# Attention in quarter-array matmuls: scores as 64 x 32, the product with v as 64 x 64, without zero padding

## The chip, the cores and the metric

The kernel runs on one core of a Trainium2 chip. A core has TensorE for matrix multiplication (its matmul side is called PE in the rows, its weight loads PEld), VectorE (DVE), ScalarE (ACT), GpSimd (POOL) and SyncE (SP), which issues the DMAs. TensorE writes to PSUM, which has eight banks of 512 fp32 columns on 128 partitions; the other engines read the results from there. The metric is the time of one execution in microseconds (us), and lower is better. Three executions of the kernel before took 828.35, 829.13 and 830.47 us; the median is 829.13.

## The reference

Attention over 4 batches, 8 heads, 576 positions and 64 dimensions a head, then two dense layer pairs on 2304 tokens of 512:

```python
scores = scale * np.matmul(q, k.transpose(0, 1, 3, 2))
rel = pos[:, None] - pos[None, :]
mask_plain = (rel >= 0) & (rel < 32)
mask_dil = (rel >= 0) & (rel < 128) & (rel % 4 == 0)
# heads 0 to 3 use mask_plain, heads 4 to 7 use mask_dil
scores = np.where(masks, scores, -1e9)
attn = np.exp(scores - max); attn = attn / (sum + 1e-09)
x = np.matmul(attn, v)                    # then (2304, 512)
x = elu(x @ w_in) @ w_out                 # 512 -> 2048 -> 512
x = h * clip(h + 3, 0, 6) / 6 @ w2_out    # h = x @ w2_in
```

A query sees only 32 keys, either the last 32 or every fourth of the last 128. All is fp32.

## The kernel before

**Units.** Attention is cut into 18 units of 128 tokens with all eight heads. The host lays the queries out in blocks of 32 rows, each with a window of 64 keys: four blocks of consecutive positions for the plain heads and four blocks of every fourth position for the dilated ones, eight blocks (`NB`) for each of four heads of a kind. A block of one head is thus 32 queries by 64 keys by 64 dimensions. The kernel packs them into larger matmuls with zeros: the 128 rows of `q` hold two heads' dimensions, with the two heads' queries in different columns and zeros in between, so that one matmul of 128 rows gives two heads' scores (64 columns of queries, 64 of keys). `scores` (L571) makes 16 such matmuls into one bank `ps`. `low` (L583) scales and masks them on VectorE, `top` (L591) takes the row minimum, `expos` (L611) the exponentials on ScalarE, `norm` and `scale` (L619, L623) divide by the sum. `turn` (L626) transposes the result in four TensorE transpositions into a bank `pp`. `turned` (L633) copies it to `pt` in two halves of 64 partitions, each into other columns; the rest of `pt` was set to zero once (L1499) and stays zero. `pv` (L642) multiplies with `v`, again 16 matmuls on 128 rows, into a bank `po`, which `x_hi` and `x_lo` (L655, L658) read out as a high and a low part, or `whole` (L719) for the last six units.

**The first four units** take another way through the same steps (`full`, `pe_masks`): the mask is added in the bank by bf16 matmuls with `minus`, a scaled identity (`masked`, L564), and the maximum and the difference are taken from PSUM (`less`, L597).

**The two layer pairs.** `tile1` (L764) runs the first pair on 512 tokens at a time: a block of 12 matmuls of 128 x 512 into a bank h0 or h1 (`gemm1`, L752), the ELU on ScalarE and VectorE, and 12 matmuls into the four banks y0 to y3 (`g2`, L806). They need three passes each, since every number is split into two fp32r parts. The last 768 tokens of the first pair and all of the second run later (L1109, L1163, L1353) and read nothing of attention's banks or buffers. The weights are loaded as raw 64-bit numbers and converted on ScalarE and VectorE (L335 to L377), and weight sums of the second pair are formed beside the first one's matmuls.

**The order** is made by a planner (L108 to L196). Each piece of work is a job with a key, a table of costs by engine and what it needs; the planner keeps a clock for each engine, picks for each the ready job with the lowest key unless a later one starts earlier by its cost, and emits it. Rings of slots stand for buffers: a job that takes a slot waits for the planned end of the slot's last users. Scores, transposition and product of a unit each take one bank in turn, by `bank_tags` (L513): in the first four units from a0, a1 and y0 to y3, later from the ring "a" (a0 and a1) alone. The first four units stand at the start, the next four among the first 512 tokens' matmuls, the other ten behind. What an engine does is in this fixed order; at run time it waits on semaphores. Until 46 us of its clock the planner fills TensorE's idle time with matmuls of the identity (`fill`, L1484).

Of the kernel before, what the change touches and what calls it, by code (L numbers as in the profile page):

```python
# [42 lines left out]
    LEAD=10.0,  # L43
# [6 lines left out]
    BUFS=dict(y=4, ghl=3, q=1, k=1, v=1, pt=1, g=8, w=6, o=9),  # L50
# [16 lines left out]
class Slot:  # L67

    def __init__(self, tag=None):
        self.tag, self.users = tag, ()  # L70

# [127 lines left out]
def tile_window_attention_two_mlps(  # L199
# [45 lines left out]
    mask = at.tile([P, 5, KW], BF16, name="mask")  # L245
# [17 lines left out]
    RINGS = {n: Ring(SIZES.get(n, 1)) for n in (*SIZES, "p0", "p1")}  # L263
# [4 lines left out]
    RINGS["all"] = Ring(list(BANKS.values()))  # L268
    RINGS["ghl"] = Ring([Slot(f"ghl{n}") for n in range(SIZES["ghl"])])
# [242 lines left out]
    pts = [at.tile([P, NB // 2, HH, 2 * QB], F32, name=f"pt{z}") for z in range(SIZES["pt"])]  # L512
    bank_tags = deque(["a", "y0", "a", "y1", "y2", "y3"])  # L513
# [6 lines left out]
    def unit(u, key, step):  # L520
# [3 lines left out]
        for n, src, shape, us, dk in (  # L524
            ("q", q_in, [P, 2, NB, KW], 1.3, 0), ("k", k_in, [P, k_in.shape[2]], 1.1, 0),
# [13 lines left out]
        masks = [first_seen(u * QB, S // DIL)] * DIL + [first_seen(u * UN + n * QB, S) for n in range(UN // QB)]  # L539
        tags = []  # L540
        for _ in range(3):
            tags.append(bank_tags[0] if u < U1 else "a")
            bank_tags.rotate(-1)
        r = {}

        def bank(k, shape, nm):
            r[nm] = ps.tile(shape, F32, tag=bu[k].tag, name=f"{nm}{u}")
            return r[nm]

        def window(n):  # L550
            if n < DIL:
                return t["k"][:, 2 * (UN + WIN):].rearrange("p (c r z) -> p c r z", c=2, r=DIL)[:, :, n]
            n -= DIL
            return t["k"][:, 0:2 * (UN + WIN)].rearrange("p (c z) -> p c z", c=2)[:, :, n * QB:n * QB + KW]

        runs = []
        while sum(w for _, w, _ in runs) < NB:
            n = sum(w for _, w, _ in runs)
            runs.append((n, next(w for w in range(NB - n, 0, -1) if len(set(masks[n:n + w])) == 1), masks[n]))

        full = u < CFG["FULL"]
        pe_masks = u < CFG["MPE"]

        def masked(e):  # L564
            pe = bank(0, [P, NB, KW], "ps")
            for n, w, z in runs:
                nc.tensor.matmul(
                    pe[:, n:n + w, :], minus, mask[:, z:z + 1, :].to_broadcast([P, w, KW]), start=(n == 0), stop=False
                )

        def scores(e):  # L571
            pe = r["ps"] if pe_masks else bank(0, [P, NB, KW], "ps")
# [3 lines left out]
            for n in range(NB):  # L576
                kk = window(n)
                for c in range(2):
                    nc.tensor.matmul(
                        pe[c * KW:(c + 1) * KW, n, :], t["q"][:, c, n, :], kk[:, c], start=not pe_masks, stop=not pe_masks or n == NB - 1  # L580
                    )

        def low(e):  # L583

            for n, w, z in runs:
                nc.vector.scalar_tensor_tensor(
                    out=r["s"][:, n:n + w, :], in0=r["ps"][:, n:n + w, :], scalar=-SCALE,
                    in1=mask[:, z:z + 1, :].to_broadcast([P, w, KW]), op0=ALU.mult, op1=ALU.add,
                )

        def top(e):  # L591
            if pe_masks:
                nc.vector.tensor_reduce(out=r["mx"], in_=r["ps"], axis=AX.X, op=ALU.max)
# [3 lines left out]
        def less(e):  # L597
            nc.vector.tensor_tensor(
                out=r["s"], in0=r["ps"], in1=r["mx"].to_broadcast([P, NB, KW]), op=ALU.subtract
            )  # L600
# [10 lines left out]
        def expos(e):  # L611
            x, z = (r["ps"], SCALE) if pe_masks else (r["s"], -1.0)
            for n in range(NB):
                nc.scalar.activation(  # L614
                    out=r["s"][:, n, :], in_=x[:, n, :], func=AF.Exp, scale=z, bias=r["mx"][:, n],
                    accum_out=r["sm"][:, n],
# [9 lines left out]
        def turn(e):  # L626
            pp = bank(1, [P, NB // 2, P], "pp")
            for m in range(0, NB, 2):
                nc.tensor.transpose(pp[:, m // 2, :], r["s"][:, m:m + 2, :].rearrange("p n k -> p (n k)"), ident)

        pt = pts[u % len(pts)]

        def turned(par):  # L633
            def fn(e):
                rows = slice(par * KW, (par + 1) * KW)
                copy(
                    e, pt[rows, :, :, par * QB:(par + 1) * QB],
                    r["pp"][rows].rearrange("p m (h i) -> p m h i", i=QB),
                )
            return fn  # L640

        def pv(e):  # L642

            po = bank(2, [P, KD, UN], "po")
            for m in range(NB // 2):
                for h in range(HH):
                    o = po[h % 2 * D:(h % 2 + 1) * D]
                    if m < DIL // 2:
                        o = o[:, 2 + h // 2].rearrange("p (i r) -> p r i", r=DIL)[:, 2 * m:2 * m + 2]
                    else:  # L650
                        n = 2 * m - DIL
                        o = o[:, h // 2, n * QB:(n + 2) * QB]
                    nc.tensor.matmul(o, t["v"][:, m, h, :], pt[:, m, h, :], start=True, stop=True)  # L653
# [978 lines left out]
```

## Time and profile before

| | |
|---|---|
| median of three runs | 829.13 us |
| the profiled execution | 829.3 us, span 827.6 us |
| PE busy | 811.6 us (98%) |
| DVE, ACT busy | 636.3 us (77%), 505.5 us (61%) |
| DMA | 230.49 MB, mean 279 GB/s |
| first matmul of the first layer | 29.47 us |
| last product with v | begins at 278.49 us |

The busy time of PE counts each matmul to its modelled end, and neighbours overlap, so that gaps shorter than a matmul's drain don't show in it. The chain of waits shows from start to start instead. Names are those of the program: `ps` scores, `pp` transposed exponentials, `pt` their copy, `po` product with v, `h` and `yp` the banks of the first layer pair. A line can be that of a helper: L276 is every copy, L279 every difference, L335 to L346 the conversion of raw weights. The granted clock was 1.00 in all stretches.

### The profile page before, as it was taken

The numbers are of one execution on the slowest core, as the hardware profiler recorded it, in microseconds if no ns is written. First come the engines' busy times: TensorE is split into PE (matmuls) and PEld (weight loads), VectorE is DVE, ScalarE is ACT, GpSimd is POOL, SyncE is SP. The second block draws the span as 40 slices with busy tenths as digits, with TensorE's granted clock in tenths as the row PEclk, the third lists the DMA queues.
The fourth block names the chain that finished last, engine by engine and source line by source line (L and its number), as shares of the span: only waits on it lengthen the run. The fifth ranks groups of instructions, "written<-read, shape, count | busy, mean of one in ns | idle before, by whom it ended". The sixth has DMA issues, their size and how long they took to land.

```text
span 827.6 us, 15806 instructions
## 1 busy us (share of the span) xinstructions
PE 811.6 (98%) x5691; PEld 750.5 (91%) x5691; DVE 636.3 (77%) x1310; ACT 505.5 (61%) x1179; POOL 47.6 (6%) x71
## 2 busy tenths in 40 slices
PE   8899999999999999999999999999999999999998
PEld 7788888888877887999999999999999999999998
DVE  5999898877778787677998675797677896555985
ACT  2999975766676655677786554444555445444452
POOL 2000010001001000100000000100001100002001
PEclk9999999999999999999999999999999999999999
DMA  9999557866888736999779998986999915778323
GB/s 355 408 408 367 195 180 246 271 213 228 261 287 294 243 125 216 397 414 401 266 256 339 392 373 312 400 339 179 343 379 355 389 59 171 255 256 291 96 59 121
DMA packets 89550, 230.49 MB, mean 279 GB/s; under 512 B 9344, under 2 KB 24192, under 8 KB 89472
## 3 DMA queue, kind: packets, MB, share of 16 engines
q1 hardware_dynamic: 89328, 229.35, 77.8%
q8 instruction: 45, 0.74, 0.4%
q14 instruction: 33, 0.27, 0.1%
q10 hardware_dynamic: 144, 0.13, 0.0%
HBM read 163.38 MB, written 66.06 MB: 277 GB/s over the span
## 4 chain that ended last, share of the span: by engine, by line
PE 78%; DMA 10%; DVE 4%; ACT 4%; issue 1%; SPq 1%; DVEq 0%; ACTq 0%
PE m L1353 20%; PE cq L1163 15%; PE h L757 11%; PE yp L812 9%; PE yl L1109 8%; PE cr L1163 7%; PE cp L1163 4%; DMA raw<-in_w_in_dram 3%; DMA w2do<-store__95 2%; ACT s L614 1%; DMA w2do<-stg 1%; PE po L653 1%; PE m_1x L1353 1%; DMA w2di<-store__95 1%; DMA ws_e<-w2de 1%
## 5 line engine op out<-in xcount | busy, mean ns | idle before, releaser
L812 PE MATMUL yp<-ghl,w 128*128 128x512 f32 x576 | 141.0, 393 | 0.0
L812 PEld LDWEIGHTS yp<-ghl,w 128*128 128x128 f32 x576 | 106.6, 188 | 22.6
L757 PE MATMUL h<-xh,w 128*128 128x512 f32 x384 | 125.6, 394 | 0.1
L1163 PE MATMUL cq<-x,ws_i 128*128 128x384 f32 x576 | 113.3, 339 | 0.7 <-ACT t L276 0.6
L1163 PEld LDWEIGHTS cq<-x,ws_i 128*128 128x128 f32 x576 | 100.9, 188 | 1.4 <-ACT t L276 1.1
L1353 PE MATMUL m<-w,gc 128*128 128x256 f32 x792 | 100.2, 281 | 0.0
L1353 PEld LDWEIGHTS m<-w,gc 128*128 128x128 f32 x792 | 97.2, 190 | 0.0
L757 PEld LDWEIGHTS h<-xh,w 128*128 128x128 f32 x384 | 72.0, 188 | 15.5 <-DVE e L790 0.3
L276 ACT CAST gc<-g 128x384 fp32r<-128x384 f32 x96 | 49.2, 514 | 41.8 <-PE m L1353 22.1
L757 PE MATMUL h<-xl,w 128*128 128x512 f32 x192 | 73.3, 389 | 0.0
L276 ACT COPY t<-cq 128x384 f32<-128x384 f32 x96 | 45.7, 476 | 38.9 <-PE cq L1163 38.0
L1209 ACT ACTIVATE g<-t 128x384 f32<-128x384 f32 x72 | 37.8, 525 | 49.0 <-DVE t L1199 49.0
L1109 PE MATMUL yl<-gl,w 128*128 128x384 f32 x384 | 67.4, 334 | 0.0
L1109 PEld LDWEIGHTS yl<-gl,w 128*128 128x128 f32 x384 | 66.7, 188 | 0.0
L279 DVE TENSOR_TENSOR gc<-g,gc 128x384 fp32r<-128x384 f32 x85 | 48.2, 569 | 17.8 <-ACT gc L276 16.6
L276 ACT CAST gc<-gf 128x384 fp32r<-128x384 f32 x72 | 37.0, 514 | 39.7 <-PE m L1353 35.9
L1215 DVE SCALAR_TENSOR_TENSOR g<-g,t 128x384 f32<-128x384 f32 x72 | 40.2, 559 | 26.6 <-ACT g L1209 26.1
L1163 PE MATMUL cr<-x,ws_i 128*128 128x384 f32 x288 | 55.7, 339 | 0.0
L1353 PE MATMUL m<-ws_e,gc 128*128 128x256 f32 x384 | 52.3, 282 | 0.8 <-DMA ws_e<-w2de 0.8
L335 ACT ACTIVATE raw<-raw 128x512 f32<-128x512 f32 x64 | 42.5, 683 | 17.1 <-DMA raw<-in_w_out_dram 11.6
L1199 DVE TENSOR_TENSOR t<-cr,t 128x384 f32<-128x384 f32 x64 | 35.6, 556 | 20.1 <-ACT t L276 17.9
L1163 PEld LDWEIGHTS cr<-x,ws_i 128*128 128x128 f32 x288 | 50.9, 188 | 0.0
(139 smaller groups left out, 1450.6 us busy)
## 6 DMA issues: line engine op xcount, KB each, us to landing
ws_i<-w2di SPq DMA_DIRECT2D x84, 512.0 KB, 5.5
raw<-in_w_in_dram SPq DMA_DIRECT2D x32, 512.0 KB, 8.0
raw<-in_w_out_dram SPq DMA_DIRECT2D x32, 512.0 KB, 6.5
ws_l<-w2dl SPq DMA_DIRECT2D x28, 512.0 KB, 7.3
ws_e<-w2de SPq DMA_DIRECT2D x24, 512.0 KB, 4.3
w2di<-store__95 SPq DMA_DIRECT2D x44, 256.0 KB, 4.8
rhs<-stg SPq DMA_DIRECT2D x28, 384.0 KB, 6.0
x<-rhs SPq DMA_DIRECT2D x28, 384.0 KB, 8.4
```

What stands on the lines that cost most here:

```text
L276: (nc.scalar.copy if e == "A" else nc.vector.tensor_copy)(out=out, in_=in_)
L279: ENG[e].tensor_tensor(out=out, in0=in0, in1=in1, op=ALU.subtract)
L335: nc.scalar.activation(out=x, in_=x, func=AF.Prelu, scale=2.0 ** -112, alpha=-2.0 ** 32)
L614: nc.scalar.activation(out=r["s"][:, n, :], in_=x[:, n, :], func=AF.Exp, scale=z, bias=r["mx"][:, n], accum_out=r["sm"][:, n],)
L757: nc.tensor.matmul(h, w[:, a, c * P:(c + 1) * P], x[b][:, c, :], start=n == 0, stop=n == len(steps) - 1,)
L812: nc.tensor.matmul(ys[b, n], w[:, a, n * P:(n + 1) * P], g[:, c, :], start=(i == 0 and s == 0), stop=(i == KF - 1 and s == 2),)
L1109: nc.tensor.matmul(ys["l", t, n], w_t[0, i, 1][:, a, n * P:(n + 1) * P], r["g"][:, v], start=i == 0 and s == 0, stop=i == KF - 1 and s == 2,)
L1163: nc.tensor.matmul(r[b], w[:, a, p * P:(p + 1) * P], x2[c, k, p][:, z, :], start=start and p == 0 and n == 0, stop=p == 1 and n == 2, skip ...
L1199: nc.vector.tensor_tensor(out=r[n], in0=r[b], in1=r[n], op=ALU.add)
L1209: nc.scalar.activation(out=g_t[c, j][:, k, t].rearrange("q i n -> q (i n)"), in_=r[src], func=AF.Relu, bias=3.0)
L1215: nc.vector.scalar_tensor_tensor(out=z, in0=z, scalar=6.0, in1=r[src], op0=ALU.min, op1=ALU.mult)
L1353: nc.tensor.matmul(ms[c, k, i], r["z"][:, a, i * P:(i + 1) * P], w[:, v, :], start=(c, nm) in opened, stop=end and s == 2,)
```

## The change

Each head's block is its own matmul, on a part of the array. `q` has no zeros and half the columns. Scores: 32 matmuls on 64 rows (one head's dimensions, `z` says which half) and 32 columns (a block's queries, at one of four column places), with 64 keys streamed; the two row halves write to two banks. Product with v: 32 matmuls of 64 rows (64 keys, the plain ones in the lower and the dilated ones in the upper half) by 64 columns, with 32 queries streamed, again into two banks. A unit therefore takes a pair of adjacent banks for its scores and one for its product, and one bank for the transposition. Pairs are a0 and a1, y0 and y1, y2 and y3 for the first four units, and only a0 and a1 later. PSUM becomes one tensor with areas. The transposed exponentials stand as the product needs them, so one copy of 128 x 512 into one of two `pt` buffers replaces two of 64 x 512 (in the first four units, two copies of 128 x 256). The masks are laid out anew, with four pieces more copied by GpSimd before the first masked matmul and three after it.

```diff
-    LEAD=10.0,
+    LEAD=10.0, TS=0.85, TP=1.1,
...
-    BUFS=dict(y=4, ghl=3, q=1, k=1, v=1, pt=1, g=8, w=6, o=9),
+    BUFS=dict(y=4, ghl=3, q=1, k=1, v=1, pt=2, g=8, w=6, o=9),
...
+    PAIRS = [Pair(x, BANKS[x], BANKS[x[0] + str(int(x[1]) + 1)]) for x in ("a0", "y0", "y2")]
+    RINGS["six"] = Ring([s for x in PAIRS for s in x.slots])
+    RINGS["pairs"], RINGS["pair"] = Ring(PAIRS), Ring(PAIRS[:1])
+    psum_ = ps.tile([P, len(BANKS), DM], F32, name="psum_")
...
-    pts = [at.tile([P, NB // 2, HH, 2 * QB], F32, name=f"pt{z}") for z in range(SIZES["pt"])]
-    bank_tags = deque(["a", "y0", "a", "y1", "y2", "y3"])
...
-            ("q", q_in, [P, 2, NB, KW], 1.3, 0), ("k", k_in, [P, k_in.shape[2]], 1.1, 0),
+            ("q", q_in, [P, 2, NB, QB], 0.65, 0), ("k", k_in, [P, k_in.shape[2]], 1.1, 0),
...
+        blocks = [(m, c, par) for m in range(MB) for c in range(2) for par in range(2)]
...
         def masked(e):
-            pe = bank(0, [P, NB, KW], "ps")
-            for n, w, z in runs:
-                nc.tensor.matmul(
-                    pe[:, n:n + w, :], minus, mask[:, z:z + 1, :].to_broadcast([P, w, KW]), start=(n == 0), stop=False
-                )
+            pe = r["ps"] = bank(0, KW)
+            for z in range(2):
+                for k, (n, w, v) in enumerate(runs):
+                    nc.tensor.matmul(
+                        pe[:, z, n, :], minus, mask[:, v:v + 1, :].to_broadcast([P, w, KW]), start=k == 0, stop=False
+                    )
...
         def scores(e):
...
-            for n in range(NB):
-                kk = window(n)
-                for c in range(2):
-                    nc.tensor.matmul(
-                        pe[c * KW:(c + 1) * KW, n, :], t["q"][:, c, n, :], kk[:, c], start=not pe_masks, stop=not pe_masks or n == NB - 1
-                    )
+            for m, c, par in blocks:
+                for kind in range(KINDS):
+                    n = 2 * m + par
+                    for z in range(2):
+                        rows, o = slice(z * D, (z + 1) * D), (2 * c + par) * QB
+                        nc.tensor.matmul(
+                            pe[o:o + QB, z, 2 * m + kind, :], t["q"][rows, c, kind * DIL + n, :], window(kind, n)[rows, c],
+                            start=not pe_masks, stop=not pe_masks or m == MB - 1 and kind == 1,
+                            tile_position=(z * D, o),
+                        )
...
+        HALF_T = 2 if full else 1
...
-                rows = slice(par * KW, (par + 1) * KW)
-                copy(
-                    e, pt[rows, :, :, par * QB:(par + 1) * QB],
-                    r["pp"][rows].rearrange("p m (h i) -> p m h i", i=QB),
-                )
+                w = NB // 2 // HALF_T
+                copy(e, r["pt"][:, n * w:(n + 1) * w], r["pp"][:, n * w:(n + 1) * w])
...
         def pv(e):
-            po = bank(2, [P, KD, UN], "po")
...
-                    nc.tensor.matmul(o, t["v"][:, m, h, :], pt[:, m, h, :], start=True, stop=True)
+            po = bank(2, UN)
+            for m, c, par in blocks:
+                n = 2 * m + par
+                for kind in range(KINDS):
+                    for z in range(2):
+                        rows = slice(kind * KW, (kind + 1) * KW)
+                        o = po[z * D:(z + 1) * D, kind, c]
...
+                        nc.tensor.matmul(
+                            o, t["v"][rows, n, 2 * c + z, :], r["pt"][rows, z * MB + m, (2 * c + par) * QB:(2 * c + par + 1) * QB],
+                            start=True, stop=True, tile_position=(kind * KW, z * D),
+                        )
...
+        pairs, single = (RINGS["pairs"], RINGS["six"]) if u < U1 else (RINGS["pair"], RINGS["a"])
+        take1 = [(pairs, bu[0])]
...
+        for h in range(HH):
+            rows = slice(h * QB, (h + 1) * QB)
+            nc.gpsimd.tensor_copy(out=mask[rows, 4], in_=mask[rows, 1 - h % 2])
```

The planner then makes another order. On TensorE, in the full stretch (`po` is the tenth unit's product with v, `ps` the eleventh's scores, `yp` a second-layer block), the kernel before has:

```order
L653 MATMUL po_1875<-pt_96,v_1670 64x2x32 x8
L653 MATMUL po_1875<-pt_96,v_1670 64x64 x8
L579 MATMUL ps_1898<-k_1780,q_1778 64x64 x16
L812 MATMUL yp_0_1687<-ghl_3_1865,w_3_1_754 128x512 x3
L812 MATMUL yp_1_1691<-ghl_3_1865,w_3_1_754 128x512 x3
```

The changed kernel, at a like place between the ninth and the tenth unit (every output is `psum_`; L688 is the product with v, L857 the second layer, L610 the scores, L802 the first layer):

```order
L688 MATMUL psum__96<-pt_1936,v_1665 64x32 x32
L857 MATMUL psum__96<-ghl_1_1921,w_1_1_728 128x512 x12
L610 MATMUL psum__96<-k_1846,q_1843 32x64 x32
L802 MATMUL psum__96<-xh_850,w_3_0_748 128x512
L802 MATMUL psum__96<-xl_851,w_3_0_748 128x512
```

A second-layer block has come between the product and the next scores. There are six such neighbours in the full stretch before, and none after.

On ScalarE at the start (`s` the exponentials, `pt` the copies of the transposed ones, `xh` the high part of the product, `raw` the first weights), the kernel before has:

```order
L603 ACTIVATE s_196<-s_196 128x512
L276 COPY pt_96<-pp_264 64x16x32 x2
L603 ACTIVATE s_230<-s_230 128x512
L276 CAST xh_314<-po_294 128x4x128
L276 COPY pt_96<-pp_326 64x16x32
L603 ACTIVATE s_269<-s_269 128x512
L276 CAST xh_314<-po_353 128x4x128
L335 ACTIVATE raw_0_0_188<-raw_0_0_188 128x512
```

and the changed one:

```order
L639 ACTIVATE s_205<-s_205 128x512
L639 ACTIVATE s_248<-s_248 128x512
L304 COPY pt_348<-psum__96 128x256 x2
L304 CAST xh_389<-psum__96 128x4x128
L639 ACTIVATE s_313<-s_313 128x512
L304 COPY pt_438<-psum__96 128x256 x2
L363 ACTIVATE raw_0_0_160<-raw_0_0_160 128x512
L367 ACTIVATE raw_0_0_160<-raw_0_0_160 128x512
```

The copies are half as wide and all on ScalarE, the second unit's exponentials come before the first one's copies, and the first weights come up ahead of the second unit's cast.

## Rows read from the trace of the kernel before

**Rows 1.** The page's first part: busy us, share of the span, instructions.

```profile
PE 811.6 (98%) x5691; PEld 750.5 (91%) x5691; DVE 636.3 (77%) x1310; ACT 505.5 (61%) x1179; POOL 47.6 (6%) x71
```

**Rows 2.** Windows: us; busy PE, PEld, DVE, ACT, POOL; PEclk; DMA share; GB/s.

```profile
30.00:80.00 50.00, 50.00 (x356) 40.47 (x355) 46.86 (x92) 48.75 (x122) 0.00 (x0) 1.00 1.02 395
...
230.00:283.00 53.00, 51.57 (x419) 42.03 (x420) 40.26 (x87) 37.30 (x106) 5.55 (x7) 1.00 0.81 270
```

**Rows 3.** Chain of waits, 46 to 157 us: start, us to the next, what.

```profile
54.84 1.08 PE ps L579 x32
...
55.93 2.95 PE yp L812 x12
...
66.08 2.72 PE h L757 x12
...
154.91 1.08 PE po L653 x32
...
155.99 0.93 PE ps L579 x32
...
156.93 2.94 PE yp L812 x12
```

**Rows 4.** Tiles ps and po: count, duration ns min/median/max, first and last start, forms.

```profile
L579 PE MATMUL ps<-k,q x576: 222/222/270, 5.6 to 266.6; 128*64 128x64 f32 x192
...
L653 PE MATMUL po<-pt,v x576: 222/222/270, 13.4 to 279.4; 128*64 128x64 f32 x192
```

**Rows 5.** Windows of 30 ns, scores (L579) alone: passes under way in brackets.

```profile
54.77:54.80 0.03, 0.03 (x2) 0.03 (x2) 1.00 1.79 683
...
54.86:54.89 0.03, 0.03 (x4) 0.03 (x5) 1.00 0.69 273
...
54.92:54.95 0.03, 0.03 (x6) 0.03 (x6) 1.00 0.70 273
...
54.98:55.01 0.03, 0.03 (x8) 0.03 (x6) 1.00 0.68 273
```

**Rows 6.** Timeline, fills on TensorE: start, us, engine, line, operation, count.

```profile
9.43 1.83 PE L1493 MATMUL fill<-ident 128*128 128x128 f32 x14
```

**Rows 7.** TensorE's waits by releaser: us in total, times, longest.

```profile
PE po L653 <- ACT pt L276: 1.9, 3, 1.2
PE po L653 <- DVE pt L276: 1.7, 1, 1.7
```

**Rows 8.** Tile pp: the copies of the transposed exponentials.

```profile
L276 ACT COPY pt<-pp x33: 561/581/587, 11.7 to 276.5; 64x512 f32<-64x512 f32 x33
...
L276 DVE COPY pt<-pp x3: 694/695/695, 17.0 to 229.9; 64x512 f32<-64x512 f32 x3
```

**Rows 9.** Timeline of the start.

```profile
3.42 0.23 POOL L1461 TENSOR_SCALAR_AFFINE_SELECT mask<-mask 32x64 bf16<-32x64 bf16 x1
...
4.90 0.81 PE L567 MATMUL ps<-mask,minus 128*128 128x320 bf16 x4
...
6.84 0.69 DVE L593 TENSOR_REDUCE st<-ps 128x8 f32<-128x512 f32 x1 [4.84 <-PE ps L579]
...
20.62 0.68 ACT L335 ACTIVATE raw<-raw 128x512 f32<-128x512 f32 x1 [1.01 <-DMA raw<-in_w_in_dram]
...
28.84 0.58 ACT L276 CAST xh<-po 128x512 fp32r<-128x512 f32 x1
...
29.47 0.72 PE L757 MATMUL h<-xh,w 128*128 128x512 f32 x2
```

**Rows 10.** The page's groups: a copy of 384 columns on ScalarE.

```profile
L276 ACT COPY t<-cq 128x384 f32<-128x384 f32 x96 | 45.7, 476 | 38.9 <-PE cq L1163 38.0
```

**Rows 11.** DMA issues: count, KB each, median us to landing.

```profile
q<-in_q_dram SPq DMA_DIRECT2D x18, 512.0 KB, 6.4
```

**Rows 12.** Timeline, 62 to 65 us: a product and its last reader.

```profile
61.99 1.15 PE L653 MATMUL po<-pt,v 128*64 128x64 f32 x32
...
64.03 0.69 DVE L660 TENSOR_TENSOR xl<-po,xh 128x512 fp32r<-128x512 f32 x1
```

More of the change, by code (lines that the diff above doesn't have):

```diff
@@ L1 @@
-from collections import deque
 from contextlib import ExitStack
@@ L550, in window @@
-        def window(n):
-            if n < DIL:
+        plain = [first_seen(u * UN + n * QB, S) for n in range(UN // QB)]
+        masks = [z for m in range(MB) for z in ({(0, 0): 0, (1, 0): 4}[tuple(plain[2 * m:2 * m + 2])], first_seen(u * QB, S // DIL))]
+        runs = []
+        while sum(w for _, w, _ in runs) < NB // 2:
+            n = sum(w for _, w, _ in runs)
+            w = next(w for w in range(NB // 2 - n, 0, -1) if len(set(masks[n:n + w])) == 1)
+            runs.append((slice(n, n + w), w, masks[n]))
@@ L557, in unit @@
-        while sum(w for _, w, _ in runs) < NB:
-            n = sum(w for _, w, _ in runs)
-            runs.append((n, next(w for w in range(NB - n, 0, -1) if len(set(masks[n:n + w])) == 1), masks[n]))
         full = u < CFG["FULL"]
         pe_masks = u < CFG["MPE"]
+        flat = lambda x: x.rearrange("p e m k -> p e (m k)")
+        assert all(w == 1 or v == 0 and w == NB // 2 for _, w, v in runs)
+        wide = lambda x: x.rearrange("p (e m) k -> p e m k", e=2)
         def masked(e):
-            pe = bank(0, [P, NB, KW], "ps")
-            for n, w, z in runs:
-                nc.tensor.matmul(
-                    pe[:, n:n + w, :], minus, mask[:, z:z + 1, :].to_broadcast([P, w, KW]), start=(n == 0), stop=False
-                )
+            pe = r["ps"] = bank(0, KW)
[4 more added lines that the diff above has]
+                    )
@@ L640, in turned @@
+            for m in range(NB // 2):
+                nc.tensor.transpose(r["pp"][:, m, :], r["s"][:, 2 * m:2 * m + 2, :].rearrange("p n k -> p (n k)"), ident)
+        HALF_T = 2 if full else 1
+        def turned(n):
+            def fn(e):
+                if "pt" not in r:
+                    r["pt"] = take(at, "pt", [P, NB // 2, P], F32, f"pt{u}")
+                w = NB // 2 // HALF_T
+                copy(e, r["pt"][:, n * w:(n + 1) * w], r["pp"][:, n * w:(n + 1) * w])
             return fn
@@ L1463, in make_mask @@
         later(1, WIN)
+        for h in range(HH):
+            rows = slice(h * QB, (h + 1) * QB)
+            nc.gpsimd.tensor_copy(out=mask[rows, 4], in_=mask[rows, 1 - h % 2])
     def make_masks(e):
+        for n in range(3):
+            nc.gpsimd.tensor_copy(out=mask_[:, n], in_=mask[:, 0])
         later(3, QB // 2)
@@ L1490, in fill @@
         tag = RINGS["h"].take(())
-        y = ps.tile([P, P], F32, tag=tag, name=f"fill{next(turns)}")
+        y = area(tag, P)
         for _ in range(n):
```

136 lines of the change are left out of this document (73 added, 63 removed).

## The prediction

> **What bounds the kernel now.** I read the page's busy table first. The matmul side of TensorE is busy 811.6 of 827.6 us and ScalarE 505.5 [rows 1]: TensorE sets the time unless a stage shows otherwise. The table by stage was next, because a matmul is recorded as busy while it drains. From 30 to 80 us TensorE has no idle time at all, while ScalarE is busy 48.75 and VectorE 46.86 of 50 us; from 230 to 283 us TensorE idles 1.43 of 53 us [rows 2]. The chain of waits between 46 and 157 us then shows what attention costs there, since its pieces run from one start to the next. A block of scores takes 1.08 us, and the second layer's block behind it 2.95 us where one without a neighbour takes 2.72 (the 2.72 us of a first-layer block is the same length): 1.08 + 0.23 = 1.31 us a block. Where a product with v is followed at once by the next unit's scores, the two take 1.08 + 0.93 and again 0.22 behind them: 2.23 us, not 2.62. Side by side they save 0.39 us, the ends of one block [rows 3].
>
> So 14 of the 18 units (those behind the first four) stand in a full queue of TensorE, where a microsecond of matmul is a microsecond of the end; the first four are a chain over four engines ahead of the first large matmul, at 29.47 us. Nothing behind 283 us is touched but the places of buffers.
>
> **The blocks.** Every program matmul of fp32 shows as two passes: 576 for 18 units, 32 a block, 222 ns each [rows 4]. A block's 32 passes take 1.15 us, so the 31 steps between starts take (1.15 - 0.22) / 31 = 30 ns in the mean. The 30 ns windows show that they are no single file: two are under way in the first window, four 90 ns later, six at 150 ns, eight at 210 ns [rows 5]. Two start together, one on each half of the columns, and 60 ns later the next two. The fills, on all 128 columns, take (1.83 - 0.27) / 13 = 120 ns a pass [rows 6]. So a pass lasts 60 ns with 64 columns and 120 with 128; for 32 I estimate 30. In all of these the stationary operand is as wide as the moving one, so no row says which of the two sets it.
>
> The change doubles the matmuls: 32 a block, 64 passes, in both blocks. Scores load 32 columns and stream 64. They come in eight groups of four, two matmuls on one tile and two, between them, on the tile in the other half of the rows. If a matmul starts when its tile is free, in program order, the first pair of a group runs beside the second pair of the group before, and a group adds two passes: 8 x 0.12 + 0.12 = 1.08 us if the streamed columns set a pass, 8 x 0.06 + 0.06 = 0.54 if the loaded ones do. Before it is 8 x 0.12 = 0.96. The product with v loads 64 columns and streams 32, in eight groups on four tiles: 8 x 2 x 0.03 = 0.48 by the streamed ones, 8 x 2 x 0.06 = 0.96 by the loaded ones. Together, against 1.92 before: 1.56 by the streamed, 1.50 by the loaded, 2.04 if the longer of the two sets each. That is -0.36, -0.42 or +0.12 us a unit. If the row halves don't run side by side, all 128 passes follow each other at 30 ns: 3.84, +1.92. I take -0.30, near the two that agree and a little towards the third: 14 x -0.30 = **-4.2 us**. (The plan books 0.85 and 1.1 us for the new blocks; that sets its order and measures nothing.)
>
> The Trainium skill, TensorEngine Tiling (Array Packing), section Instruction Overhead, speaks against half of this: each matmul carries some 60 cycles, one of 1 column lasts as long as one of 60, and a tiling factor should not be taken from a side that is already small. By it the 32 streamed columns of the product with v save nothing and its 0.48 would be 0.96. No row here has a matmul of under 64 columns. If it holds, the unit gains by the scores alone.
>
> **The neighbours that part.** The old order has six places in the full stretch where a product with v is followed at once by the next unit's scores. In the new one there is none: both blocks take a pair of banks, these units have only the pair a0, a1, and the next scores wait until the product is read out, so one second-layer block stands between. The two shapes differ too. Each lost neighbourhood costs the 0.39 us above: 6 x 0.39 = **+2.3 us**.
>
> **The wait for the copies.** Before the product with v, TensorE waited 1.9 us in three places for ScalarE's copies and 1.7 in one for a VectorE copy [rows 7]. The last, at 230 us, is the second of two copies, put on another engine. Now it is one copy of the same length on 128 rows into one of two buffers: of two copies of 0.58 us a unit [rows 8] one goes, 14 x 0.58 us. I take back 1.0 of the 1.7 (**-1.0 us**; ends 0 and -1.7), for a copy can still queue.
>
> The scores' pass on VectorE goes from 23 instructions to 29 (nine of 512 columns, five units with four of 128); it lies beside the two blocks that stand between scores and transposition, 5.4 us, and costs nothing while VectorE keeps up.
>
> **The start.** Later: GpSimd copies four pieces of mask more, at 0.23 us, ahead of the first masked matmul (+0.9), and ten masked matmuls stand ahead of the first scores where four took 0.81 us, with fewer columns in all (taken as +0.4). Earlier: eight copies at some 0.58 us on ScalarE (one on VectorE, 0.69) become eight of 256 columns. From 0.476 at 384 columns and 0.581 at 512 I estimate 0.37: 7 x 0.58 - 8 x 0.37 = 1.1 us of ScalarE and 0.69 of VectorE [rows 8 to 10]. The loads of q halve: four times 256 KB by the first weights, at 395 GB/s 2.7 us earlier [rows 2, 11], and the 1.0 us that ScalarE waited for the first weights goes. The chain runs over VectorE, nearly gapless from 6.84 us, and over ScalarE's cast at 28.84 us. Added 1.3, taken away up to 0.69 + 1.1 + 1.0 = 2.8, of which perhaps two thirds lie on the chain: **-0.5 us**, ends -1.5 and +1.2.
>
> **Sum.** The profiled execution took 829.3 us (span 827.6, 1.7 around it), 0.2 above the median of the three runs, 829.13. 829.3 - 4.2 + 2.3 - 1.0 - 0.5 = 825.9; I say **825.8**. Its own range, with the ends -5.9 and +1.7 of the blocks (14 x -0.42, 14 x +0.12), 0 and -1.7, and -1.5 and +1.2: 822.5 to 834.5.
>
> **Rivals.**
> - *The longer operand sets each pass.* For it: the 60 and 120 ns steps fit it as well as the others. Against: nothing yet. 14 x 0.12 + 2.3 - 1.0 - 0.5 = +2.5: 831.8.
> - *Single file.* The halves of the rows share something and the passes follow at the 30 ns of today. For it: no row shows row halves. Against: column halves do run side by side [rows 5]. 28 blocks x 0.96 = 26.9, with 2.3, and 1.9 for two blocks on the start's chain: 829.3 + 31.1 - 0.5 = 860. It decides early: of 2.3 - 1.0 - 0.5 = 0.8 us are left to pay, so the change is slower than before unless the two blocks together shrink by 0.06 us a unit. The skill's page TensorE: Matmul & The Clock Gate, section "Wait — 56ns, not 53.3ns?", has a floor of 25 ns between starts, however small the matmul; were it one for all tiles, 64 passes would take 1.6 us, 0.64 more than now, and the time would be some 850. The starts in twos [rows 5] speak against it across tiles.
> - *The pair is read out late.* Scores wait until VectorE has read the last product out of the pair. At 62 us the last reader ends at 64.72, 1.58 us behind the product's end at 63.14 [rows 12]; the second-layer block between takes 2.94, so 1.36 us are spare. If VectorE queues over 1.4 us longer, each unit waits; at 1 us, 14 more: 829.3 + 14 + 2.3 - 4.2 - 0.5 = 841.
> - *The gain is lost.* VectorE at 94% and ScalarE at 98% from 30 to 80 us [rows 2] may be late next, and then TensorE waits for what it gained, and the parted neighbours cost nothing either. Against: ScalarE loses copies. Only the start stays: 828.8.
>
> **How the numbers follow.** Forecast 0.54, longer operand 0.12, single file 0.11, late pair 0.05, gain lost 0.18. A measurement of this kernel can tell 0.3% (2.5 us) from no change: under 826.6 is faster, over 831.6 slower. Of the forecast 0.43 lies below 826.6 and the rest within; of the lost gain 0.02 is faster; the longer operand falls in two, 0.05 within and 0.07 slower; the other two are slower. Faster 0.45, same 0.32, slower 0.23. The range leaves out the single file and the far end of the late pair above, some 0.05 below: 822 to 838.
>
> **What would show it.** Right: a block of scores between 0.6 and 1.1 us and one with v between 0.6 and 1.1 in the chain, with two tiles or more starting together; 0.2 us behind every one; no wait of TensorE before the scores for VectorE; the first large matmul near 29 us. The first step fails if a block takes 1.2 us or more; the second if blocks lose nothing by standing alone; the forecast as a whole if TensorE idles from 230 to 283 us more than today's 1.43 us.

## The result, and the profile after

The changed kernel takes 837.85 us (median of six runs, 836.32 to 838.19) where the kernel before took 829.80 beside it: a ratio of 1.0084, interval 1.0055 to 1.0113. It is slower, by 8 us; 825.8 was forecast. The profiled execution took 837.98 us, its span is 835.8 us, 8.2 more than the 827.6 of before.

Three places in the span say where. The first large matmul starts at 33.63 us instead of 29.47 [rows 9]: +4.2. The last matmul of the first layer starts at 328.85 instead of 325.72: the long stretch between gave back 1.0. The end is 8.2 later, so the stages behind, where no operation of TensorE is new, lost 5.1.

The page's first part and its third, of the kernel after (busy us, share, instructions; then a DMA queue's packets, MB, share):

```profile
PE 817.1 (98%) x6842; PEld 751.8 (90%) x6842; DVE 635.9 (76%) x1316; ACT 489.2 (59%) x1153; POOL 59.6 (7%) x89
...
q8 instruction: 54, 0.88, 0.4%
```

The same row of the third part, before:

```profile
q8 instruction: 45, 0.74, 0.4%
```

TensorE has 1151 matmul passes more, and as many loads of operands [rows 1]. The queue named "instruction" carries its code: 0.88 MB in 54 packets is 16 KB each, and 2 x 6842 instructions over 54 are 253 (before 2 x 5691 over 45: 253). A piece of code is then some 256 instructions of TensorE, with the few that are neither a pass nor a load; the borders below are exactly 256 apart. I had read this part of the page and not asked what it meant for a kernel that doubles them.

The chain of waits of the kernel after, 46 to 75 us (start, us to the next, what), answers to [rows 3]:

```profile
58.08 0.95 PE psum__96 L610 x56
59.02 2.95 PE psum__96 L857 x12
61.97 2.72 PE psum__96 L802 x12
...
70.60 1.06 PE psum__96 L688 x64
71.67 2.95 PE psum__96 L857 x12
```

Scores take 0.95 us instead of 1.08, the product with v 1.06 instead of 1.08, and behind each the 2.95 us block stands as before. Windows of the kernel after (us; busy PE, PEld, DVE, ACT, POOL; clock; DMA share; GB/s): the last stretch of [rows 2], the first layer from its first large matmul to its last, and what lies behind it up to TensorE's end:

```profile
230.00:283.00 53.00, 52.69 (x590) 42.42 (x590) 38.37 (x86) 36.67 (x107) 5.68 (x6) 1.00 0.78 268
...
33.63:328.85 295.22, 293.83 (x2903) 237.96 (x2900) 243.97 (x517) 207.13 (x550) 24.15 (x27) 1.00 0.72 247
...
330.00:400.00 70.00, 65.39 (x351) 61.59 (x350) 52.52 (x113) 48.33 (x110) 5.09 (x6) 1.00 1.01 397
400.00:832.36 432.36, 428.83 (x2924) 426.98 (x2922) 321.34 (x653) 220.08 (x469) 23.23 (x22) 1.00 0.74 262
```

The same parts of before:

```profile
29.47:325.72 296.25, 293.56 (x2035) 239.86 (x2036) 242.98 (x511) 214.91 (x561) 13.34 (x16) 1.00 0.75 259
325.72:330.00 4.28, 3.13 (x15) 2.30 (x13) 3.85 (x9) 2.37 (x6) 0.90 (x1) 1.00 0.68 214
330.00:400.00 70.00, 68.96 (x380) 66.98 (x381) 51.75 (x111) 51.76 (x117) 3.21 (x4) 1.00 0.99 389
400.00:824.13 424.13, 421.84 (x2886) 420.36 (x2884) 317.37 (x644) 222.16 (x474) 24.45 (x23) 1.00 0.76 270
```

Between the first and the last large matmul of the first layer TensorE's idle time falls from 2.69 to 1.39 us. From 330 to 400, with the DMA engines full in both, it grows from 1.04 to 4.61, but before has another 1.15 just ahead of 330 us, where after has none. And the start, in the timeline of TensorE after (start, us, what, count, in brackets the idle time before it and what ended it):

```profile
15.02 1.14 PE L688 MATMUL psum__96<-pt,v 64*64 64x32 f32 x64
...
17.37 0.66 PE L665 MATMUL psum__96<-ident,s 128*128 128x128 f32 x4
17.96 0.47 PE L610 MATMUL psum__96<-k,q 64*32 64x64 f32 x27
20.10 0.75 PE L610 MATMUL psum__96<-k,q 64*32 64x64 f32 x37 [1.67 <-issue]
20.78 1.93 PE L688 MATMUL psum__96<-pt,v 64*64 64x32 f32 x64
...
24.54 0.85 PE L688 MATMUL psum__96<-pt,v 64*64 64x32 f32 x18
26.48 1.50 PE L688 MATMUL psum__96<-pt,v 64*64 64x32 f32 x46 [1.09 <-issue]
...
32.68 1.01 PE L610 MATMUL psum__96<-k,q 64*32 64x64 f32 x64
```

Twice TensorE stops in the middle of a block, on operands that it already has, and no event ends the wait. Counting its instructions in the trace from the first, it stops behind number 705 and number 961: 256 apart. The packets of the instruction queue run from 17.76 to 18.84 and from 24.01 to 25.09 us: TensorE goes on 1.26 and 1.39 us after they land. One of them, in a window of the DMA view from 17.7 to 18.9 us:

```profile
q8 instruction: 1, 0.02, 5.6%
```

Not all of the 4.2 us comes from these stops. VectorE's first maximum, at 6.84 us in [rows 9], starts at 8.45 after, and the second unit's transposition at 17.37 instead of 15.68, both ahead of the first stop. The first line is VectorE after, the second TensorE before:

```profile
8.45 0.69 DVE L629 TENSOR_REDUCE st<-psum__96 128x8 f32<-128x512 f32 x1 [8.45 <-PE psum__96 L610]
...
15.68 0.66 PE L629 MATMUL pp<-ident,s 128*128 128x128 f32 x4
```

The granted clock is the third thing that [rows 9] had not: from 20.5 us on it is 0.50, the lower of the two levels, 1.2 GHz. It falls right behind the idle 1.67 us, and a product with v then takes 1.93 us. The window of the kernel after:

```profile
20.50:30.50 10.00, 8.91 (x164) 8.24 (x152) 5.61 (x11) 4.05 (x8) 0.00 (x0) 0.50 0.94 371
```

### The profile page after: what moved, and what is told of

Its sections match the earlier page's. It is cut to its first block, busy times and chain, and to the rows that moved or that the text cites. A ratio compares the mean times of both kernels' runs of the same rounds, so it can differ in the third digit from the quotient of the medians.

```text
span 835.8 us, 18116 instructions
## 1 busy us (share of the span) xinstructions
PE 817.1 (98%) x6842; PEld 751.8 (90%) x6842; DVE 635.9 (76%) x1316; ACT 489.2 (59%) x1153; POOL 59.6 (7%) x89
## 4 chain that ended last, share of the span: by engine, by line
PE 73%; DMA 14%; DVE 6%; ACT 3%; issue 2%; SPq 1%; POOL 1%; DVEq 0%; POOLq 0%; ACTq 0%
PE psum__96 L1208 23%; PE psum__96 L1398 19%; PE psum__96 L857 12%; PE psum__96 L802 12%; PE psum__96 L1154 3%; DMA ws_e<-w2de 2%; DMA raw<-in_w_out_dram 2%; DMA ws_i<-w2di 2%; PE psum__96 L688 2%; PE psum__96 L610 2%; DMA ws_l<-w2dl 1%; DMA w<-w2do 1%; DMA x<-rhs 1%; DMA w2db<-store__95 1%; PE psum__96 L665 1%
## 5 line engine op out<-in xcount | busy, mean ns | idle before, releaser
L1208 PE MATMUL psum__96<-x,ws_i 128*128 128x384 f32 x1008 | 184.0, 339 | 1.8 <-DMA ws_i<-w2di 1.5
L1208 PEld LDWEIGHTS psum__96<-x,ws_i 128*128 128x128 f32 x1008 | 176.2, 188 | 2.9 <-DMA ws_i<-w2di 2.1
L857 PE MATMUL psum__96<-ghl,w 128*128 128x512 f32 x576 | 141.6, 394 | 0.0
L802 PE MATMUL psum__96<-xh,w 128*128 128x512 f32 x384 | 126.5, 395 | 0.7 <-DVE e L835 0.7
L857 PEld LDWEIGHTS psum__96<-ghl,w 128*128 128x128 f32 x576 | 106.3, 188 | 22.6
L1398 PE MATMUL psum__96<-w,gc 128*128 128x256 f32 x864 | 108.3, 282 | 0.4 <-DMA w<-w2do 0.4
L1398 PEld LDWEIGHTS psum__96<-w,gc 128*128 128x128 f32 x864 | 105.5, 190 | 0.6 <-issue 0.6
L802 PEld LDWEIGHTS psum__96<-xh,w 128*128 128x128 f32 x384 | 71.9, 188 | 16.6 <-DVE e L835 1.3
L802 PE MATMUL psum__96<-xl,w 128*128 128x512 f32 x192 | 73.3, 389 | 0.0
L1154 PE MATMUL psum__96<-gl,w 128*128 128x384 f32 x384 | 67.6, 334 | 0.0
```

Of the source, the lines that this page charges most:

```text
L802: nc.tensor.matmul(h, w[:, a, c * P:(c + 1) * P], x[b][:, c, :], start=n == 0, stop=n == len(steps) - 1,)
L857: nc.tensor.matmul(ys[b, n], w[:, a, n * P:(n + 1) * P], g[:, c, :], start=(i == 0 and s == 0), stop=(i == KF - 1 and s == 2),)
L1154: nc.tensor.matmul(ys["l", t, n], w_t[0, i, 1][:, a, n * P:(n + 1) * P], r["g"][:, v], start=i == 0 and s == 0, stop=i == KF - 1 and s == 2,)
L1208: nc.tensor.matmul(r[b], w[:, a, p * P:(p + 1) * P], x2[c, k, p][:, z, :], start=start and p == 0 and n == 0, stop=p == 1 and n == 2, skip ...
L1398: nc.tensor.matmul(ms[c, k, i], r["z"][:, a, i * P:(i + 1) * P], w[:, v, :], start=(c, nm) in opened, stop=end and s == 2,)
```

## The experiments

Two losses were to be explained. For the start: TensorE runs out of instructions (theory), or the new tiles, mask pieces and pairs of banks delay it, or the clock does. For the loss behind 330 us: the order that the plan wrote (theory), or the new blocks and their pairs of banks. All ratios are to the kernel before, run beside each.

**The order alone, both ways (e1, e2).** The changed kernel planned with the old block costs:

```
-    LEAD=10.0, TS=0.85, TP=1.1,
+    LEAD=10.0, TS=1.136, TP=1.056,
```

> The changed kernel, planned with the block costs of before (scores 1.136, product with v 1.056 us instead of 0.85 and 1.1): the same operations, another order. Theory (the order): the 5 to 6 us lost between 330 and 410 us come from the order that the new costs give, so they come back: 831 to 834 us, with the first large matmul still near 33.6 us. Rival (the pairs of banks or the work of the new blocks themselves lose them): 836.5 to 839.5.

841.64 us, 1.0157 (1.0133 to 1.018). Neither: worse than after, with the first large matmul at 34.35, and 4.25 us of idle TensorE from 330 to 400 us. And the kernel before planned with the new costs:

```
-            key, scores, {"T": 0.071 * 2 * NB},
+            key, scores, {"T": 0.85},
...
-        j8 = job(key + 0.7, pv, {"T": 0.066 * 2 * NB}, ...
+        j8 = job(key + 0.7, pv, {"T": 1.1}, ...
```

> The kernel before, planned with the block costs of the changed one (0.85 and 1.1 us): only its order changes. Theory (the order): it loses 4 to 7 us behind 330 us, 833 to 837, the start as before (first large matmul 29.5 us). Rival (not the order): 828.5 to 831.

826.66 us, 0.9978 (0.996 to 0.9996): faster than before, and neither guess was right. The windows of the stage, of e1:

```profile
330.00:400.00 70.00, 65.75 (x352) 63.20 (x352) 43.96 (x91) 49.70 (x108) 4.95 (x6) 0.98 0.86 314
```

and of e2:

```profile
330.00:400.00 70.00, 69.43 (x387) 67.90 (x386) 54.64 (x116) 53.82 (x119) 3.68 (x4) 1.00 1.01 393
```

The new costs as such don't cause the loss. That an order alone moves the same operations by some 3 to 4 us (4.2 more than after, 2.7 less than before) is what these two show.

**Twice the instructions, with the old blocks (e3).** In the kernel before, each matmul of the first four units is issued as two of half the streamed columns:

```
+    for x in ((0, 1) if u < U1 else (None,)):
+        y = slice(None) if x is None else slice(x * QB, (x + 1) * QB)
         nc.tensor.matmul(pe[c * KW:(c + 1) * KW, n, y], t["q"][:, c, n, :], kk[:, c, y], ...)
```

(and the product with v in the same way).

> The kernel before, with each matmul of scores and of the product with v of the first four units issued as two of half the streamed columns: the same work and tiles, 128 instead of 64 instructions a block, 512 more in all. Theory (the supply of instructions: TensorE's come in pieces of 256, one in about 6 us while the DMA engines are full): idle time of TensorE that no engine ends, first large matmul 3 to 8 us later than 29.5 (two pieces more), total 832 to 838. Rival (masks, pairs or tiles on row halves delay the changed kernel's start): eight blocks up to 0.3 us longer, first large matmul 29.5 to 31, total 829 to 831.5.

833.63 us, 1.0049 (1.0023 to 1.0075), the first large matmul at 34.41. The numbers are the theory's, but not its mechanism. Timeline of TensorE:

```profile
13.74 2.08 PE L581 MATMUL ps<-k,q 128*64 128x32 f32 x64
...
16.07 2.08 PE L660 MATMUL po<-pt,v 128*64 128x32 f32 x64
```

A pass that streams 32 columns instead of 64 takes as long: (2.08 - 0.22) / 63 = 30 ns, the 30 of [rows 4, 5]. So a block took twice as long, and TensorE, that much slower, stood still on "issue" once only, for 0.29 us. For the start this run decides nothing. It settles what the prediction left open: streaming fewer columns than are loaded saves nothing.

**Fewer instructions in the fills (e4).** The changed kernel, its fills of 128 columns issued as a quarter as many of 512:

```
-        y = area(tag, P)
-        for _ in range(n):
-            nc.tensor.matmul(y, ident, ident, start=True, stop=True)
+        y = area(tag, 4, P)
+        four = ident.rearrange("p (a k) -> p a k", a=1).to_broadcast([P, 4, P])
+        for _ in range(n // 4):
+            nc.tensor.matmul(y, ident, four, start=True, stop=True)
+        for _ in range(n % 4):
+            nc.tensor.matmul(y[:, 0], ident, ident, start=True, stop=True)
```

> The changed kernel with its fill matmuls in the start four times as long and a quarter as many (some 88 TensorE instructions fewer before the first large matmul, the same busy time). Theory (supply of instructions): a third of a piece less, first large matmul 1.5 to 3 us earlier than 33.6, the stalls of 1.67 and 1.09 us later in the program or gone, total 835 to 836.5. Rival (the chain over VectorE and ScalarE, or the fills themselves, set the start): first large matmul within 0.5 us of 33.6, total 837.5 to 838.5.

835.01 us, 1.0077 (1.0052 to 1.0102); the first large matmul at 33.82. The theory's forecast for the start failed: that matmul came where the rival had it. The rival's total, 837.5 to 838.5, didn't come either. How the start failed is the best sight of the supply so far. Timeline of TensorE:

```profile
16.91 0.95 PE L610 MATMUL psum__96<-k,q 64*32 64x64 f32 x57
20.56 0.41 PE L610 MATMUL psum__96<-k,q 64*32 64x64 f32 x7 [2.69 <-issue]
...
23.51 1.51 PE L688 MATMUL psum__96<-pt,v 64*64 64x32 f32 x48
26.88 0.65 PE L688 MATMUL psum__96<-pt,v 64*64 64x32 f32 x16 [1.87 <-issue]
```

It stops behind numbers 705 and 961 again (and for 0.53 us behind 449), at another place of the program, waits longer, and goes on at 20.56 and 26.88, where after goes on at 20.10 and 26.48. The pieces come when they come; arriving earlier at a border only lengthens the wait.

**The first four units as before (e5).** The other 14 keep the new form:

```
         for u in range(U1):
-            unit(u, CFG["ATT0"] + CFG["K0"] + u * CFG["KS"], 0)
+            unit0(u, CFG["ATT0"] + CFG["K0"] + u * CFG["KS"], 0)
```

(unit0 is the unit of before, with its padded q and its own v from two more inputs; the two tiles of transposed exponentials lie in its one.)

> The changed kernel, but the first four units (those ahead of the first large matmul) take the form of before: 32 matmul passes a block, padded q, two copies of the exponentials into the zero-padded tile, the mask pieces of the new form built later. The other 14 units stay changed. Theory (TensorE runs out of instructions in the start, and its clock falls after that): no idle time of TensorE that nothing ends, the granted clock full throughout, the first large matmul at 29 to 30.5 us, total 832 to 835. Rival (the later stages take up what the start gains, since they wait for loads): first large matmul the same, total 836 to 838.5.

834.78 us, 1.0078 (1.0052 to 1.0103): the start is back, the total hardly: 6.0 us over before, where after is 8.05 over. Timeline of TensorE at its end:

```profile
29.62 1.67 PE L1044 MATMUL psum__96<-xh,w 128*128 128x512 f32 x6 [0.42 <-ACT xh L308]
```

The clock stays at the upper level to 469 us and nothing waits on "issue". But this is another order too, and it idles elsewhere: 4.1 us from 460 to 520, where after idles 1.6.

**The same operations in other orders (e6, e7, e8, e10).** Three variants with the old start and one of the changed kernel as it is; each differs in due times or costs of the plan alone:

```
e6:  PREP0=130 -> 140, PREP1=-10 -> -20, PREPL=(60, 140) -> (50, 130)
e7:  TS=0.85 -> 1.0, PREP0=130 -> 110, PREPL=(60, 140) -> (50, 130)
e10: TS=0.85 -> 1.0, UL=14 -> 15, PREP1=-10 -> -20
e8:  BIAS=0.6 -> 0.8   (the changed kernel, new start)
```

> As the kernel with the old start, with three due times of the weights' preparation moved (pieces of the last weights 10 us earlier, of the others 10 us later at one end and 10 earlier at the other): the same operations in another order. Theory (what the changed kernel loses between 330 and 400 us lies in the written order): TensorE idles under 2 us there instead of 4.6, total 826 to 830. Rival (it lies in the changed blocks or their pairs of banks): it idles 4 us or more there, total as with the old start alone, 832 to 835.

> As the kernel with the old start, with block costs 1.0 and 1.1 us in the plan and the preparation of weights 20 us and 10 us earlier: another order again. Theory (the written order): TensorE idles under 3 us between 330 and 400, total 826 to 831. Rival (blocks and pairs): 832 to 836.

> The kernel with the old start, block costs 1.0 and 1.1 us in the plan, the late units 15 instead of 14 us apart, the last weights prepared 10 us earlier. Theory (start and order are all that the change loses; the blocks themselves win little): first large matmul at 29.5, total 825 to 828.5, against 828.7 to 829.8 of before. Rival (the order's gain was luck of one plan): 830 to 834.

> The changed kernel as it is, start and all, with one number of the plan changed (a bias by which VectorE's work is offered to ScalarE, 0.8 instead of 0.6 us): the same operations in another order. Theory (of the 8.2 us lost, some 4 lie in the start and stay, some 4 in the order behind 330 us and go): first large matmul at 33.6 us still, TensorE idle under 3 us from 330 to 400 instead of 4.6, total 832 to 835. Rival (the start's delay comes back as waits behind 330, whatever the order): 836.5 to 839.

e6: 827.02 us, 0.9982 (0.9969 to 0.9995). e7: 827.00, 0.9991 (0.9973 to 1.0009). e10: 831.05, 1.0032 (1.0017 to 1.0047): its theory (825 to 828.5) failed, its rival had 830 to 834. e8: 831.18, 1.0038 (1.002 to 1.0056), below its theory's 832 to 835: by one number 2.5 us over before instead of 8.05, with the first large matmul still at 33.57. Windows of e6:

```profile
30.00:330.00 300.00, 300.00 (x2935) 244.24 (x2934) 251.11 (x533) 214.81 (x568) 26.65 (x29) 1.00 0.77 262
330.00:400.00 70.00, 68.48 (x382) 66.77 (x381) 54.56 (x115) 53.29 (x120) 1.62 (x2) 1.00 1.00 386
```

and of e8:

```profile
330.00:400.00 70.00, 67.08 (x367) 64.56 (x367) 52.62 (x111) 52.11 (x117) 3.30 (x4) 1.00 1.01 393
```

With all the new blocks of the full stretch in place, e6 has no idle TensorE at all in 300 us and 1.5 in the stage behind; e8 has 2.9 there, with the new start as well. So the loss behind 330 us doesn't follow from the blocks or the pairs of banks. e6 beats both kernels, by 0.2% over before. That gain isn't shown to be the change's: e2, the old operations in another order, is as far ahead.

**A block repeated, with the DMA engines nearly idle (e9).** In the changed kernel the last unit's two blocks are issued 12 times over:

```
-            for m, c, par in blocks:
+            for m, c, par in blocks * (12 if u == NU - 1 else 1):
```

> The changed kernel, in which the last unit's block of scores and its product with v are each issued 12 times over (the same values again), near 272 and 284 us, where the DMA engines are a third busy. Theory (TensorE's instructions come a piece of 256 at a time, the next one being asked for when a piece is entered, and even then some 3.8 us from asking to the first instruction: 1.6 + 0.9 + 1.3): after the first pieces 3.8 us for two blocks, each series 18 to 23 us, with idle time that nothing ends exactly 256 instructions apart, total 852 to 860. Rival (pieces are late only where the DMA engines are full): 12 x 0.96 and 12 x 1.06, 11.5 to 13 us a series, without idle time, total 858 less 838 only from the blocks themselves: 859 to 862 is ruled out, 857 to 861 belongs to the first theory, 860 with series of 12 us to neither; by the rival the total is 838 + 11 x 0.96 + 11 x 1.06 = 860 at most, and 852 if the later stages take some of it up. So the series' lengths and the idle time decide, not the total.

The series of scores runs from 270.13 to 291.4 us, that of products from 303.8 to 325.8: 21 and 22 us, not 12. (The total, of a single run, is 878.08 us: some 40 more than after, about what two such series add, and outside the 852 to 860 that was forecast. The totals in the expectation don't tell the two apart and aren't used.) Timeline of TensorE:

```profile
270.13 2.60 PE L610 MATMUL psum__96<-k,q 64*32 64x64 f32 x204
275.21 2.04 PE L610 MATMUL psum__96<-k,q 64*32 64x64 f32 x128 [2.49 <-issue]
278.94 2.49 PE L610 MATMUL psum__96<-k,q 64*32 64x64 f32 x128 [1.69 <-issue]
282.67 2.49 PE L610 MATMUL psum__96<-k,q 64*32 64x64 f32 x128 [1.24 <-issue]
...
307.96 2.06 PE L688 MATMUL psum__96<-pt,v 64*64 64x32 f32 x128 [1.73 <-issue]
311.41 7.37 PE L688 MATMUL psum__96<-pt,v 64*64 64x32 f32 x256 [1.39 <-issue]
```

and a window of the scores:

```profile
276.00:291.00 15.00, 9.60 (x511) 8.99 (x497) 0.00 (x0) 0.00 (x0) 0.00 (x0) 0.51 0.02 4
```

128 passes are 256 instructions, and TensorE starts a new lot every 3.5 to 4 us, though the DMA engines move 4 GB/s. (The clock has fallen to the lower level, which draws 128 passes of scores out to 2.49 us; that is still less than the time between lots. In the series of products it isn't: from 311.41 us on 256 passes take 7.37, so there the lower clock alone nearly fills the time, and the series of scores decides.) In both series each packet starts 1.0 to 2.0 us behind the entry into the piece before its own, so it seems to be asked for then and no sooner. TensorE enters one at 275.21, the next packet runs from 276.39 to 277.69, TensorE goes on at 278.94. That is 1.2 + 1.3 + 1.25 us. In the start of after, with the engines 0.94 to 1.06 busy, the first part is 3.2 to 3.9 us (entered at 14.55 and 20.10, packets from 17.76 and 24.01), the whole 5.5 to 6.4.

**The count alone (e11).** The kernel e10, old start, each fill issued as four of 32 by 32, some 420 instructions more:

```
-        for _ in range(n):
-            nc.tensor.matmul(y, ident, ident, start=True, stop=True)
+        for _ in range(4 * n):
+            nc.tensor.matmul(y[:QB, :QB], ident[:, :QB], ident[:, :QB], start=True, stop=True)
```

> The last kernel (old start), with each fill matmul of the start issued as four of 32 by 32: some 420 TensorE instructions more before the first large matmul, nothing else. Theory (the count of instructions is what delays the start): pieces of 256 land about 6 us apart from 12.7 us on, idle time that nothing ends at their borders, first large matmul at 31 to 33.5, total 828 to 832. Rival (the new blocks' tiles, masks or pairs delay it): first large matmul within 0.5 us of 29.5, total as the last kernel's.

833.78 us, 1.0069 (1.0047 to 1.0092). Timeline of TensorE:

```profile
10.18 1.96 PE L1785 MATMUL psum__96<-ident 128*32 128x32 f32 x56
...
20.73 0.92 PE L940 MATMUL psum__96<-pt__97,v 128*64 128x64 f32 x25 [0.96 <-issue]
...
26.95 0.60 PE L1785 MATMUL psum__96<-ident 128*32 128x32 f32 x13 [0.89 <-issue]
...
33.18 0.45 PE L621 MATMUL psum__96<-k,q 64*32 64x64 f32 x18 [1.77 <-issue]
33.56 2.74 PE L1044 MATMUL psum__96<-xh,w 128*128 128x512 f32 x6
```

and its window of the clock:

```profile
20.50:30.50 10.00, 8.48 (x209) 7.56 (x208) 8.25 (x15) 7.48 (x13) 0.00 (x0) 1.00 1.03 406
```

The old start, with a higher count (and fills that take little longer, 1.96 us where e10 has 1.83), stops behind numbers 705, 961 and 1217, for 3.6 us in all, and its first large matmul comes at 33.56 instead of e10's 29.26, though the clock is at its upper level all the while. So the supply alone can cost a start about 4 us; the tiles, mask pieces and pairs aren't needed for that, nor is the lower clock. That this is within 0.1 us of after's 33.63 is chance. In after the two stops are 2.8 us, 1.6 to 1.7 us of delay stand ahead of them, and the lower clock follows the first; how its 4.2 divides among the three isn't shown. That all of it goes with the new form of the first four units is: with the old form of these units (e5) it starts at 29.62.

## Why the prediction was wrong

That 837.85 lies just inside the stated 822 to 838 is luck: the terms alone reached 834.5, and the late pair, which stood for the rest, did not come.

*The start, -0.5 forecast, +4.2 measured.* This is the step that failed most: "Added 1.3, taken away up to 2.8". The 1.3 came (1.6 at VectorE's first maximum); what was to be taken away doesn't show at the first large matmul, and more was added. It priced what VectorE, ScalarE and GpSimd do, and took TensorE's 1151 passes more as free but for their own time. Of these 256 lie in the first four units (4 x 2 x 32): with their loads 512 instructions, two pieces of code. Up to 35 us a piece takes 5.5 to 6.8 us, and TensorE needs more of them than come. Even the end of +1.2 was reckoned without it. The Trainium skill, Runtime: NRT & Kernel Launch, section Instruction fetch mechanics, names the 16 KiB blocks and calls the crossing of a border "mostly hidden". The traces agree on the size and on fetching beside the work, not on the rest: 0.3 to 2.7 us of standstill at a border here. By the page's rule this term would have kept its -0.5.

*The blocks, -0.30 a unit forecast, -0.15 measured in the chain.* The range of this term held it (-0.42 to +0.12), the value was wrong: 14 x 0.15 = 2.1 us, not 4.2. The rival "the longer operand sets each pass" has the right sum, 2.04 us for the two blocks where the chain has 0.95 + 1.06 = 2.01, but its mechanism is shown for half of it. e3 shows that 32 streamed columns behind 64 loaded ones save nothing, and the product with v agrees: its passes start in fours, 58 ns apart. e11 has 32 by 32 on one tile: (1.96 - 0.20) / 55 = 32 ns a pass (0.20 us is a single one), where the fills of [rows 6] take 120. For scores the rival fails. Their passes start two by two, at first 27 ns apart, and 33 of the 64 start in the first 0.28 us, where four of its eight groups take 4 x 0.12 = 0.48; the other 31 take 0.52 us more. So 32 loaded columns seem to shorten a pass in the first half of the block; what slows the second half stays open. Windows of after, scores (first three) and product (passes begun in brackets):

```profile
58.00:58.06 0.06, 0.05 (x4) 0.06 (x7) 1.00 1.08 427
...
58.00:58.29 0.29, 0.28 (x33) 0.28 (x34) 1.00 1.01 399
58.00:58.82 0.82, 0.81 (x64) 0.81 (x64) 1.00 1.03 413
...
70.52:70.64 0.12, 0.11 (x8) 0.11 (x8) 1.00 1.00 410
```

The Trainium skill's rule that a factor should not be taken from a side that is already small (TensorEngine Tiling (Array Packing), Instruction Overhead) said of the product with v that its 32 streamed columns save nothing, and the trace agrees: 1.08 to 1.06.

*The single file is out.* (1.01 - 0.22) / 63 = 12.5 ns a pass for scores, (1.14 - 0.22) / 63 = 14.6 for products, in the mean, against the 30 of a single file.

*The neighbours, +2.3.* Right in kind: each block is followed by 2.95 us, none by another block. *The wait for the copies, -1.0.* No block of the stretch waits for them any more; with the other waits between the first and the last large matmul of the layer 1.3 us went (2.69 to 1.39). Blocks, neighbours and waits make -2.1 + 2.3 - 1.3 = -1.1 there, and -1.0 is measured: this stretch is accounted for. *The pair read out late* did not come: the only wait before scores for VectorE in the stretch is 0.4 us.

*Behind 283 us, "nothing touched but the places of buffers", +5.1 measured.* The second step that failed. The plan books the blocks and lays out everything else around them. TensorE's waits from 330 to 400 us after:

```profile
PE psum__96 L1208 <- ACT t L304: 2.8, 5, 0.6
PE psum__96 L1208 <- DMA ws_l<-w2dl: 1.3, 2, 0.8
PE psum__96 L1208 <- ACT g L1269: 0.5, 1, 0.5
```

With them the idle time is 3.6 us more than before's in these 70 us. Before has 1.15 more just ahead of them, after 1.2 more behind 400 us (3.53 against 2.29), so waits make 3.7 of the 5.1; the other 1.4 I can't assign. Against the medians of before beside them, the changed operations took 8.1, 12.3 and 2.5 us more in three orders with the new start (after, e1, e8), and 6.0, -1.7, -1.7 and 2.3 in four with the old one (e5, e6, e7, e10). The order is shown to decide; what in it makes ScalarE and the loads late there is not (the DMA engines are full in that stage in after and e8, but in before, e2 and e6 as well). In the prediction this term should have stood with an estimate of zero and, going by these orders, a range of some 5 us to either side.

The forecast's own test, TensorE's idle time from 230 to 283 us, came out right (0.31 us), and a forecast can pass it and be 12 us off: it watched the one stretch that I had worked out.

## What to carry to other kernels

Count TensorE's instructions as well as its time. Where a change makes matmuls smaller and more, take 256 instructions (128 passes with their loads) and set the time that TensorE takes for them in the densest place against the time that a piece took to come here, 3.5 to 4 us with idle DMA engines and 5.5 to 6.8 with full ones: where it is shorter, TensorE stands still at the borders. Larger matmuls between the small ones hide it: after has no such stop behind 35 us, where blocks of 2.7 us stand between. And where a planner writes the order, a new cost is a new order: run a change in several orders before its worth is read off one.

## What the hardware showed

- TensorE's code arrives in pieces of 256 instructions. A piece's packet starts behind the entry into the piece before, 1.0 to 2.0 us in the repeated blocks of e9. From entering to going on it was 3.5 to 4 us with idle DMA engines, 5.5 to 6.8 with full ones (after, e4, e11). Idle time put down to "issue", inside a block, exactly 256 instructions from the last such place, is its mark.
- On one tile a pass took 32 ns with 32 columns loaded and streamed (e11), some 60 with 64 loaded, whether 64 or 32 were streamed (before, e3), 120 with 128 (before). On tiles of 64 rows the passes followed at 12.5 ns in the mean with 32 loaded and 64 streamed, at 14.6 with 64 loaded and 32 streamed (after).
- The clock fell to 1.2 GHz behind a standstill of 1.67 us in after and stayed for 10 us, with TensorE busy 8.91 of them; in e11 two standstills of 0.96 and 0.89 us, 6 us apart, left it at 2.4 GHz, and behind the third, of 1.77 us, it was at 1.2 GHz from 33.8 to 37.2 us.
